# A second pair's sorted keys crossed batch by batch, and two value products moved in their down layers

## The chip, the cores and the metric

The kernel runs on one core of a Trainium2 chip. The metric is the time of one execution on the device in microseconds (us). Three timed runs of the kernel before gave 232.80, 232.84 and 232.96 us, median 232.84.

## The reference

Attention over sorted blocks, whose result goes through a feed-forward layer:

```
P = sort_net                              # (4 batches, 8 heads, 8, 8)
5 times: P = exp(P - rowmax); P /= row sums; P /= column sums
k_sorted, v_sorted = P applied to the 8 blocks of 96 rows of k and v
scores = q_block @ k_sorted_block^T / 8   # 96 x 96 for each block
attn   = softmax(scores)                  # minus the row's maximum
x      = attn @ v_sorted_block            # -> (3072 tokens, 512)
h = x @ w_in;  g = h * cos(h);  out = g @ w_out    # 512 -> 2048 -> 512
```

q, k and v are (4, 8, 768, 64); inputs and output are float32, the matmuls run in bf16.

## The kernel before

The 3,072 tokens are eight halves n = 0 to 7 of 384 tokens; half n belongs to batch n // 2. Each half has four units u of 96 tokens, one block of all eight heads. A unit's attention is written here as (n, u). Its steps: `qk_half`, `qk` or `batch(("sc", n, u), ...)` are the scores on TensorE with maximum and subtraction on VectorE; `expo(n, u)` is the exponential on ScalarE into one of three buffers `p_buf`, followed by a transpose of the probabilities into `pT` that SP issues as a DMA (L588), or that TensorE makes later where `on_pe` is set; `av(n, u)` is the product of `pT` with the sorted values on TensorE (L625, eight matmuls) and its norm on VectorE (L636, L638); the result is turned into `xT` by a DMA from SP (L644) or, with `on_pe`, on TensorE (`x_transpose`).

The feed-forward layer of half n is `moe_up(n)`, eight steps of eight matmuls (`h`, L669) with a sine on ScalarE and a product on VectorE (`gg`) behind each, and then the down layer: three tiles of 128 tokens, each in two halves of eight matmuls into one bank (`down(n, ts, half)`, L694). In `moe_down(n, slots, mid=...)` the six halves are e = 0 to 5. Attention of later halves is written between these steps: `slots[e]` runs behind half e, `mid` behind the fourth matmul of a half, `late` behind its fifth. The order in which these calls are written is the order on every engine; nothing reorders it. So an instruction that waits holds back all that stands behind it on its engine.

The batches go in two pairs: halves 0 to 3 and halves 4 to 7. For each, keys and values are first sorted by a matmul with P (`ks`, `vs`). Sorted keys of the second pair lie in `kT2`, a view of `kTs` with 128 partitions, three places and two batches. The sort fills places 0 and 2. `k_swap` fills place 1: it carries place 0 of the upper 64 partitions to the lower 64, and place 2 of the lower 64 to the upper 64, by two DMAs from SP (L421, L422). In what follows this is the crossing. Scores read the places hp and hp + 1 together, so they need it. Halves 4 and 5 read the first batch of `kT2`, halves 6 and 7 the second. The first pair's second batch has a crossing of its own, `k_swap(kT[1])`, of half the size of that of `kT2`.

SP's queue carries the crossings, the transposes of pT and xT, the turns of queries (`q_transpose_dma`, L149) and the stores of results, in the order written. GpSimd's queue carries the loads from memory; `p_hold` and `hold` make it wait for a transpose on SP's queue before more loads go out.

PSUM tiles of the pool `big` (three of two banks) hold scores, sorts, `h` and value products in turn, so a tile is written only when the engine that read its predecessor is through.

Of the kernel before, what the change touches and what calls it, by code (L numbers as in the profile page):

```python
# [18 lines left out]
def kernel(  # L19
# [15 lines left out]
    nc = tc.nc  # L35
    B, H, S, D = q.shape
# [110 lines left out]
    def q_transpose_dma(n):  # L147
        for e in range(2):
            nc.sync.dma_start_transpose(  # L149
                out=q_of(n, e)[:, :QW].rearrange("p (x c) -> p x c", c=blk),  # L150
                in_=q_zeroed(n)[:, e * QZ:(e + 1) * QZ])
# [36 lines left out]
    kT, kT2 = [kTs[:, :, 0], kTs[:, :, 2]], kTs[:, :, :2]  # L188
# [64 lines left out]
    V, A = nc.vector, nc.scalar  # L253

    def copy_on(eng, dst, src):
        if eng is nc.scalar:
            eng.copy(dst, src)  # L257
        else:
            eng.tensor_copy(dst, src)  # L259
# [151 lines left out]
    def k_sort_g(t0, eng, pool, tag):  # L411
        ps = pool.tile([128, 4, 4 * NB], FP32, name="ks", tag=tag)
        for t in range(4):
            k_products(ps, t, t0 + t, slice(0, 128), bds[1].rearrange("p x i -> p (x i)"),
                       pair)
        copy_on(
            eng, kT2[:, ::2, :, :, t0:t0 + 4].rearrange("p e b m t -> p b e m t"),
            ps.rearrange("p t (b e m) -> p b e m t", b=2, e=2))

    def k_swap(keys):  # L420
        nc.sync.dma_start(out=keys[:64, 1], in_=keys[64:, 0])  # L421
        nc.sync.dma_start(out=keys[64:, 1], in_=keys[:64, 2])  # L422

    def hold_keys():

        nc.gpsimd.tensor_copy(held[:], kT[1][:, 1, 0, :1])
# [106 lines left out]
    def batch(*parts, between=()):  # L533

        tiles = []
        for kind, *x in parts:
            ps = big.tile([128, 2, 512], FP32, name=kind, tag="big")
            tiles.append(ps)
            if kind == "sc":
                by_half(*x, ps)  # L540
            else:
                sort_eight(kind, x[0], ps)
        step(between)
        for (kind, *x), ps in zip(parts, tiles):
            if kind == "sc":
                s_t[tuple(x)] = sp.tile([blk, 2, H2, blk], FP32, name="s", tag="s")
                qk_reduce(*x, [0, 1], ps)
            else:
                place_eight(kind, *x[:1], ps, x[1])
# [132 lines left out]
    def store(n, ts, o_s, eng=nc.sync):  # L682
        r0 = n * TC + ts * 128
        eng.dma_start(out=out[r0:r0 + 128, :], in_=o_s[:])
# [4 lines left out]
    def down(n, ts, half, stores, mid=(), late=()):  # L689
        if half == 0:  # L690
            out_ps[ts] = acc.tile([128, Dm], FP32, name="o", tag="acc")
        o = out_ps[ts]
        for f in range(half * FC // 2, (half + 1) * FC // 2):
            nc.tensor.matmul(  # L694
                o[:], gt[n, f // 4][:, f % 4, ts * 128:(ts + 1) * 128], w_out_t[:, f, :],
                start=(f == 0), stop=(f == FC - 1))
            if f % (FC // 2) == FC // 4 - 1:
                step(mid)
            if f % (FC // 2) == FC // 4:
                step(late)  # L700
        if half == 0:
            return
        if stores is None:

            z = (n % 2 * 3 + ts) * 2 * Dm
            o_s = vbuf[:, z:z + 2 * Dm].bitcast(FP32)
        else:
            o_s = op.tile([128, Dm], FP32, name="o_s", tag="o_s")
        late = n > 0 and ts == TC // 128 - 1
        copy_on(V if late else A, o_s[:], o[:])  # L710
        if stores is None or stores == "held":
            kept[n, ts] = o_s
        else:
            store(n, ts, o_s, nc.sync if late else stores)

    def step(calls):
        for f, *args in calls:
            f(*args)

    def moe_up(n, slots=()):  # L720
        for fp in range(FC // 2):
            up(n, fp)
            step(slots[fp] if fp < len(slots) else ())

    def moe_down(n, slots=(), stores=nc.sync, mid={}, late=()):

        for e in range(2 * TC // 128):
            last = e == 2 * TC // 128 - 1
            down(n, e // 2, e % 2, stores, mid.get(e, ()), late if last else ())
            step(slots[e] if e < len(slots) else ())  # L730

    B, C = (big, "big"), (acc, "acc")
# [362 lines left out]
    kse(2, V)  # L1095
    kse(1, A)
    k_swap(kT[1])
    q_transpose(2, 0, (V, V), *C)
    q_transpose(2, 1, (V, V), *B)
# [34 lines left out]
    let_go(1, 0)  # L1134
    down(1, 1, 0, nc.sync)
    k_sort_g(16, A, *B)
    down(1, 1, 1, nc.sync, mid=[(av, 2, 0, True), (expo, 2, 3, True)])
    batch(("sc", 3, 0), ("ks", 1, A))
    p_hold(2, 2)
    for z in range(3, 6):  # L1140
# [12 lines left out]
         late=[(x_transpose, 2, 3, V, *B)])  # L1153
    q_transpose_dma(4)
    moe_up(2, [[(k_next,), (qk_half, 3, 1, 0)], [(k_next,)],
               [(k_next,), (qk_half, 3, 1, 1)], [(k_next,)],
               [(k_next,), (qk_half, 3, 2, 0)], [(k_next,)],
               [(qk_half, 3, 2, 1), (k_swap, kT2)]])

    expo(3, 1)  # L1160
    expo(3, 2)
    moe_down(2, [[(ones, 1), (batch, ("sc", 3, 3), ("vs", 0, A))],
                 [(expo, 3, 3), (batch, ("vs", 1, A), ("vs", 2, A)), (av, 3, 0)],
                 [(p_hold, 3, 3), (load_q, 5), (av, 3, 1)],
                 [(batch, ("sc", 4, 0), ("vs", 3, A), ("vs", 4, A))],
                 [(expo, 4, 0), (sine_next,)]],
             mid={3: [(av, 3, 2, True)], 4: [(av, 3, 3, True)], 5: [(x_transpose, 3, 2, V, *B, 3)]})
    q_transpose_dma(5)
    hold(q_turned[1])
    load_q(6)  # L1170
    moe_up(3, [[(w_next,), (qk_half, 4, 1, 0)], [(w_next,)],
               [(w_next,), (qk_half, 4, 1, 1)], [(w_next,)],
               [(w_next,), (qk_half, 4, 2, 0)], [(w_next,)],
               [(qk_half, 4, 2, 1)], [(qk, 4, 3)]])
    expo(4, 1)
# [4 lines left out]
             None, mid={3: [(av, 4, 1)], 4: [(av, 4, 2, True)]},  # L1180
             late=[(x_transpose, 4, 2, V, *B, 3)])
# [10 lines left out]
             None, mid={3: [(qk_av, 6, 1, 5, 2)]}, late=[(x_transpose, 5, 3, V, *B)])  # L1192
# [7 lines left out]
             None, mid={3: [(qk_av, 7, 1, 6, 2)]}, late=[(x_transpose, 6, 3, V, *B)])  # L1200
# [5 lines left out]
             mid={3: [(av, 7, 2)], 4: [(av, 7, 3, True)], 5: [(x_transpose, 7, 3, A, *B)]})  # L1206
# [45 lines left out]
```

## Time and profile before

| | |
|---|---|
| median of three timed runs | 232.84 us |
| the profiled execution | 232.49 us |
| its span, first to last instruction | 230.7 us |
| TensorE matmuls, busy | 222.9 us (97%) |
| TensorE's clock granted | 1.00 |
| DMA, share of the 16 engines from 97 to 112 us | 0.97 |
| read from memory, written | 27.27 MB, 6.29 MB |

By TensorE's order the up layer 1 begins at 56.6 us and the down layer 1 at 69.7; the up layer 2 at 84.4, the down layer 2 at 96.9 and the up layer 3 at 111.7. A row of the timeline gives the start, the time from there to the group's end, the engine, the line, the operation, the operands, the count, and in brackets the idle time ahead with what ended it. A matmul's end is modelled and includes its way through the array, so rows overlap a little, and the pitch of matmuls is read from starts. "PEld" is the weight load of a matmul, which waits for its data before the matmul does. "SPq" is SP's queue; its rows tell how long the issue of a transfer took, and "DMA to landing" the time from the start of the issue to the last of its data.

### The profile page before, as it was taken

What the parts mean: (1) busy time and instruction counts of PE and PEld (TensorE: products, weight loads), DVE (VectorE), ACT (ScalarE), POOL (GpSimd) and SP (SyncE); (2) the same over time, 40 slices, a digit from 0 to 9 for tenths busy, and PEclk for the clock granted to TensorE, in tenths of its full rate; (3) what the DMA queues carried; (4) which work ended last, traced back from release to release, by engine and by line L of the source; (5) the groups of instructions that cost most, each with busy time, mean ns of one, the idle gap of its engine ahead of it and who ended that gap; (6) DMA issues with size and microseconds to landing.
All of it is one profiled execution on the core that took longest, in us unless ns stands there. A gap on an engine that the chain in (4) does not pass through costs nothing.

```text
span 230.7 us, 5533 instructions
## 1 busy us (share of the span) xinstructions
PE 222.9 (97%) x2268; PEld 138.7 (60%) x2268; DVE 170.8 (74%) x291; ACT 154.4 (67%) x207; POOL 95.9 (42%) x121
## 2 busy tenths in 40 slices
PE   8788999999999999999999999999999999999994
PEld 3377898567765566655665456555655566556553
DVE  6769968978798778877589976997699769646700
ACT  5659877777889758796688466746674667716521
POOL 7989999299960289923609000800000000000000
PEclk9999999999999999999999999999999999999999
DMA  5999999994999699897979839964934450351012
GB/s 70 226 193 207 203 207 234 196 224 150 114 121 203 171 150 137 153 160 147 162 139 86 119 74 153 211 95 73 184 123 76 91 162 0 68 146 45 0 45 94
DMA packets 67673, 31.21 MB, mean 135 GB/s; under 512 B 56384, under 2 KB 63168, under 8 KB 67392
## 3 DMA queue, kind: packets, MB, share of 16 engines
q0 software_dynamic: 24048, 13.64, 44.2%
q1 hardware_dynamic: 43312, 17.02, 35.0%
q8 instruction: 18, 0.29, 0.5%
q10 hardware_dynamic: 288, 0.20, 0.3%
q14 instruction: 7, 0.06, 0.1%
HBM read 27.27 MB, written 6.29 MB: 145 GB/s over the span
## 4 chain that ended last, share of the span: by engine, by line
PE 85%; DMA 8%; POOL 2%; DVE 2%; issue 1%; ACT 0%; ACTq 0%; POOLq 0%
PE h L669 32%; PE o L694 29%; DMA q_mem<-in_q_dram 6%; PE h L857 5%; PE o L878 5%; PE av L625 3%; PE sc L438 3%; DMA pT<-p_buf 2%; PE o L1216 2%; PE ks L408 1%; POOL w_in_t L160 1%; PE sc L504 1%; PE xps L656 1%; PE vs L449 1%; PE qps L268 1%
## 5 line engine op out<-in xcount | busy, mean ns | idle before, releaser
L669 PE MATMUL h<-xT,w_in_t 128*128 128x384 bf16 x448 | 78.4, 326 | 0.0
L694 PE MATMUL o<-w_out_t,gg 128*128 128x512 bf16 x320 | 76.0, 379 | 0.0
L673 ACT ACTIVATE c<-h,half_pi 128x768 f32<-128x768 f32 x56 | 50.5, 902 | 26.0 <-PE h L669 25.0
L677 DVE TENSOR_TENSOR gg<-c,h 128x768 bf16<-128x768 f32 x56 | 52.7, 949 | 19.5 <-ACT c L673 19.5
L669 PEld LDWEIGHTS <-w_in_t 128*128 128x128 bf16 x448 | 42.2, 98 | 26.3 <-DVE xT L259 0.6
L694 PEld LDWEIGHTS <-gg 128*128 128x128 bf16 x320 | 29.0, 99 | 28.5
L179 POOL COPY vperm<-kv 64x768 bf16<-64x768 bf16 (+2 forms) x12 | 28.3, 2408 | 4.9 <-DMA kv<-in_v_dram 4.9
L570 ACT ACTIVATE p_buf<-s 96x768 bf16<-96x768 f32 x32 | 26.6, 842 | 5.3 <-DVE s L491 4.0
L491 DVE TENSOR_TENSOR s<-sc,mx 96x384 f32<-96x384 f32 (+1 forms) x33 | 24.3, 735 | 1.6
L489 DVE TENSOR_REDUCE mx<-sc 96x4 f32<-96x384 f32 (+1 forms) x33 | 24.0, 728 | 0.4 <-PE sc L504 0.4
L638 DVE TENSOR_TENSOR xn<-av,r 96x512 bf16<-96x512 f32 x32 | 22.0, 687 | 1.1
L129 POOL DMA_DIRECT2D kv<-in_q_dram x24 | 16.0, 675 | 0.7 <-issue 0.7
L257 ACT COPY kv<-o 128x512 f32<-128x512 f32 (+2 forms) x10 | 5.2, 524 | 14.1 <-PE o L694 11.5
L257 ACT CAST kTs<-ks 128x512 bf16<-128x512 f32 (+1 forms) x18 | 11.0, 630 | 5.3 <-PE ks L408 4.4
L636 DVE RECIPROCAL r<-av 96x8 f32<-96x8 f32 x32 | 6.4, 199 | 10.0 <-PE av L625 9.5
L878 PE MATMUL o<-w_out_t,gg 128*128 128x512 bf16 x48 | 11.7, 379 | 0.0
L129 POOL DMA_DIRECT2D q_mem<-in_q_dram x16 | 10.7, 692 | 1.8 <-DMA kv<-in_v_dram 1.4
L259 DVE COPY kv<-o 128x512 f32<-128x512 f32 (+1 forms) x5 | 3.1, 611 | 11.1 <-PE o L1216 8.5
L857 PE MATMUL h<-xT,w_in_t 128*128 128x192 bf16 x128 | 11.1, 246 | 0.0
L438 PE MATMUL sc<-kTs,q_turned 128*128 128x96 bf16 x152 | 11.1, 206 | 0.0
L857 PEld LDWEIGHTS <-w_in_t 128*128 128x128 bf16 x128 | 10.5, 98 | 0.0
L596 POOL CAST held<-q_turned 96x1 f32<-96x1 bf16 x2 | 0.4, 182 | 24.3 <-DMA q_turned<-q_mem 16.9
(134 smaller groups left out, 286.0 us busy)
## 6 DMA issues: line engine op xcount, KB each, us to landing
out_dram<-kv SPq DMA_DIRECT2D x12, 256.0 KB, 2.6
out_dram<-o_s SPq DMA_DIRECT2D x10, 256.0 KB, 3.5
w_in_t<-in_moe_w_in_dram POOLq DMA_DIRECT2D x4, 512.0 KB, 11.7
w_out_t<-in_moe_w_out_dram POOLq DMA_DIRECT2D x4, 512.0 KB, 12.4
kv<-in_k_dram POOLq DMA_DIRECT2D x2, 768.0 KB, 10.0
kv<-in_v_dram POOLq DMA_DIRECT2D x2, 768.0 KB, 13.4
pair<-in_k_dram POOLq DMA_DIRECT2D x2, 768.0 KB, 12.4
kv<-in_v_dram POOLq DMA_DIRECT2D x6, 256.0 KB, 5.6
```

Source lines behind the costliest of these rows:

```text
L129: nc.gpsimd.dma_start(out=q_heads[:, i, :, e], in_=src[:, ih * IC + i, :, e])
L179: nc.gpsimd.tensor_copy(dst, src)
L489: nc.vector.reduce_max(mx[:], scv, axis=AX.X)
L491: nc.vector.tensor_tensor(s, scv, mx.to_broadcast(list(s.shape)), op=ALU.subtract)
L570: nc.scalar.activation(p[:, :, :blk], s_t.pop((n, u)).rearrange("p e h c -> p (e h) c"), AF.Exp, scale=scale)
L638: nc.vector.tensor_tensor(xn.rearrange("p h e d -> p e h d"), avv[:, :, :, :D], r.to_broadcast([blk, 2, H2, D]), op=ALU.mult)
L669: nc.tensor.matmul(h[:, f2, :w], w_in_t[:, kk, f * 128:(f + 1) * 128], xT[n][:, kk], start=(kk == 0), stop=(kk == KC - 1))
L673: nc.scalar.activation(c[:], h[:, :, :w], AF.Sin, bias=half_pi[:, 0:1])
L677: nc.vector.tensor_tensor(gt[n, fp // 2][:, f:f + 2], c[:], h[:, :, :w], op=ALU.mult)
L694: nc.tensor.matmul(o[:], gt[n, f // 4][:, f % 4, ts * 128:(ts + 1) * 128], w_out_t[:, f, :], start=(f == 0), stop=(f == FC - 1))
L857: nc.tensor.matmul(o[:, part, f2 * w:(f2 + 1) * w], w_in_t[:, kk, f * 128:(f + 1) * 128], xT[0][:, kk, h * w:(h + 1) * w], start=(kk == 0) ...
L878: nc.tensor.matmul(out_ps[ts][:], gt[0, q][:, f % 4, ts * 128:(ts + 1) * 128], w_out_t[:, f, :], start=(f == 0), stop=(f == FC - 1))
```

## The change

Three calls are written in other places, and one is split. The crossing of `kT2` becomes two calls `k_swap_b(b2)`, each with one batch, half the bytes. The first batch crosses where both crossed before, at the end of the up layer 2; the second behind the scores (4, 1) in the up layer 3. The product av(2, 0) in the down layer 1 moves from behind the fourth matmul of its half to behind the fifth; expo(2, 3) stays. The product av(3, 0) in the down layer 2 moves from the end of the second half (e = 1) to the middle of the third (e = 2).

```diff
     def k_swap(keys):
         nc.sync.dma_start(out=keys[:64, 1], in_=keys[64:, 0])
         nc.sync.dma_start(out=keys[64:, 1], in_=keys[:64, 2])
+
+    def k_swap_b(b2):
+        k_swap(kT2[:, :, b2])
...
     k_sort_g(16, A, *B)
-    down(1, 1, 1, nc.sync, mid=[(av, 2, 0, True), (expo, 2, 3, True)])
+    down(1, 1, 1, nc.sync, mid=[(expo, 2, 3, True)], late=[(av, 2, 0, True)])
     batch(("sc", 3, 0), ("ks", 1, A))
...
                [(k_next,), (qk_half, 3, 2, 0)], [(k_next,)],
-               [(qk_half, 3, 2, 1), (k_swap, kT2)]])
+               [(qk_half, 3, 2, 1), (k_swap_b, 0)]])
 
     expo(3, 1)
     expo(3, 2)
     moe_down(2, [[(ones, 1), (batch, ("sc", 3, 3), ("vs", 0, A))],
-                 [(expo, 3, 3), (batch, ("vs", 1, A), ("vs", 2, A)), (av, 3, 0)],
+                 [(expo, 3, 3), (batch, ("vs", 1, A), ("vs", 2, A))],
                  [(p_hold, 3, 3), (load_q, 5), (av, 3, 1)],
                  [(batch, ("sc", 4, 0), ("vs", 3, A), ("vs", 4, A))],
                  [(expo, 4, 0), (sine_next,)]],
-             mid={3: [(av, 3, 2, True)], 4: [(av, 3, 3, True)], 5: [(x_transpose, 3, 2, V, *B, 3)]})
+             mid={2: [(av, 3, 0)], 3: [(av, 3, 2, True)], 4: [(av, 3, 3, True)], 5: [(x_transpose, 3, 2, V, *B, 3)]})
...
     moe_up(3, [[(w_next,), (qk_half, 4, 1, 0)], [(w_next,)],
-               [(w_next,), (qk_half, 4, 1, 1)], [(w_next,)],
+               [(w_next,), (qk_half, 4, 1, 1), (k_swap_b, 1)], [(w_next,)],
                [(w_next,), (qk_half, 4, 2, 0)], [(w_next,)],
```

On TensorE in the down layer 1, where av(2, 0) begins (`pT_1510` is its turned probabilities, `o_1582` the down layer's bank; lines behind the new helper stand three further down in the changed kernel). Before:

```order
L694 MATMUL o_1582<-w_out_t_97,gg_1423 128x512
L694 LDWEIGHTS gg_1423
L694 MATMUL o_1582<-w_out_t_97,gg_1423 128x512
L625 LDWEIGHTS pT_1510
L625 MATMUL av_1602<-vS_110,pT_1510 128x65
```

And now:

```order
L697 MATMUL o_1582<-w_out_t_97,gg_1423 128x512
L697 LDWEIGHTS gg_1477
L697 MATMUL o_1582<-w_out_t_97,gg_1477 128x512
L628 LDWEIGHTS pT_1510
L628 MATMUL av_1605<-vS_110,pT_1510 128x65
```

The first matmul of the half's second four, with the weights gg_1477, now stands ahead of the product.

On TensorE in the down layer 2, where av(3, 0) begins (its turned probabilities lie in `kv_87`; `vs_2024` is the value sort ahead of it). Before:

```order
L518 MATMUL vs_2024<-bd1_152,vperm_88 96x64
L518 LDWEIGHTS vperm_88
L518 MATMUL vs_2024<-bd1_152,vperm_88 96x64
L625 LDWEIGHTS kv_87
L625 MATMUL av_2044<-vS_110,kv_87 128x65
```

And now:

```order
L697 MATMUL o_2043<-w_out_t_97,gg_1785 128x512
L697 LDWEIGHTS gg_1785
L697 MATMUL o_2043<-w_out_t_97,gg_1785 128x512
L628 LDWEIGHTS kv_87
L628 MATMUL av_2049<-vS_110,kv_87 128x65
```

The first four matmuls of the third half, with gg_1785, have gone ahead of it; the other four, with gg_1831, follow it, and av(3, 1) stands behind them as before.

On SP's queue from the crossing in layer 2 (`pT_1947`, `pT_1950` and `pT_2005` are of the units (3, 1), (3, 2) and (3, 3)). Before:

```order
L421 DMA kTs_98<-kTs_98 64x3072
L422 DMA kTs_98<-kTs_98 64x3072
L588 DMA_TRANSPOSE pT_1947<-p_buf1_108 128x8x96
L588 DMA_TRANSPOSE pT_1950<-p_buf2_109 128x8x96
L684 DMA out_0_dram<-o_s_2001 128x512
L588 DMA_TRANSPOSE pT_2005<-p_buf0_107 128x8x96
```

The same stretch now has 64x1536 in the rows L421 and L422, and is else the same. The other batch's crossing stands later on that queue, behind the turn of query half 5 and ahead of the probabilities of unit (4, 1):

```order
L687 DMA out_0_dram<-o_s_2206 128x512
L149 DMA_TRANSPOSE q_turned1_95<-kv_87 128x16x96 x2
L421 DMA kTs_98<-kTs_98 64x1536
L422 DMA kTs_98<-kTs_98 64x1536
L591 DMA_TRANSPOSE pT_2406<-p_buf2_109 128x8x96
```

Two rows are new there; no other order on SP's queue differs.

## The prediction

> **What bounds the kernel now.** I read the page first, then the chain that ended last, then the waits of TensorE, then the timeline round the two waits that the change stands beside.
>
> ```profile
> PE 222.9 (97%) x2268; PEld 138.7 (60%) x2268; DVE 170.8 (74%) x291; ACT 154.4 (67%) x207; POOL 95.9 (42%) x121
> PE 85%; DMA 8%; POOL 2%; DVE 2%; issue 1%; ACT 0%; ACTq 0%; POOLq 0%
> PE h L669 32%; PE o L694 29%; DMA q_mem<-in_q_dram 6%; PE h L857 5%; PE o L878 5%; PE av L625 3%; PE sc L438 3%; DMA pT<-p_buf 2%; PE o L1216 2%; PE ks L408 1%; POOL w_in_t L160 1%; PE sc L504 1%; PE xps L656 1%; PE vs L449 1%; PE qps L268 1%
> ```
>
> TensorE is busy for 97% of the span and carries 85% of the chain. Of DMA's 8%, 6 are the first query load, which the change doesn't touch; 2 are a transfer "pT<-p_buf", which it does. A gain can only come out of the few places where TensorE stands still. Between 70 and 112 us, the stretch that the change works in, its weight loads waited for a transfer twice:
>
> ```profile
> PEld L625 <- DMA pT<-p_buf: 1.4, 2, 0.9
> ```
>
> Both are value products (L625) that wait for their turned probabilities pT. The first is av(2,0) in the down layer 1:
>
> ```profile
> 75.90 1.03 PE L694 MATMUL o<-w_out_t,gg 128*128 128x512 bf16 x4
> 76.93 0.43 PE L625 MATMUL av<-vS,pT 96*128 96x65 bf16 x8
> 77.20 0.38 PE L694 MATMUL o<-w_out_t,gg 128*128 128x512 bf16 x1
> ```
>
> The second is av(3,1), at the end of the third half of down layer 2; av(3,0) is the group ahead of it, which the change moves:
>
> ```profile
> 101.11 0.78 PE L518 MATMUL vs<-bd,vperm 64*128 64x64 bf16 x32
> 101.88 0.42 PE L625 MATMUL av<-vS,kv 96*128 96x65 bf16 x8
> 102.14 1.89 PE L694 MATMUL o<-w_out_t,gg 128*128 128x512 bf16 x8
> 104.44 0.43 PE L625 MATMUL av<-vS,pT 96*128 96x65 bf16 x8 [0.41 <-DMA pT<-p_buf]
> 104.71 1.03 PE L694 MATMUL o<-w_out_t,gg 128*128 128x512 bf16 x4
> 105.57 0.42 PE L625 MATMUL av<-vS,pT 96*128 96x65 bf16 x8
> ```
>
> A row's duration includes the tail of its last matmul, so the pitch comes from starts. Four down matmuls from 104.71 to the next group at 105.57 take 0.86, 0.216 each. At the first place four take 75.90 to 76.93 = 1.03: **0.17 us lost**. At the second, eight from 102.14 would be through at 102.14 + 1.73 = 103.87, and av(3,1) starts at 104.44: **0.57 us lost**. These 0.74 us are all that the change can aim at.
>
> **Part 1: av(2,0) one matmul later.** Its pT lands at 76.9 (72.8 + 4.1, rows below). With five matmuls ahead of it, it starts at 75.90 + 5 x 0.216 = 76.98, just past the landing, so TensorE no longer waits: what follows comes 0.17 earlier. ScalarE's exponential, which stays at its old place, is not delayed. The product itself ends 0.05 later, which matters on VectorE, the next engine to be late:
>
> ```profile
> 77.64 0.69 DVE L638 TENSOR_TENSOR xn<-av,r 96x512 bf16<-96x512 f32 x1
> 78.55 0.95 DVE L489 TENSOR_REDUCE mx<-sc 96x8 f32<-96x768 f32 x1 [0.22 <-PE sc L504]
> ```
>
> The norm of av(2,0) will end at 78.38 instead of 78.33; the maximum behind it waits for scores that come 0.17 earlier, so it can start at about 78.40. VectorE then runs on without a wait to the transposes on which TensorE waits for it. **Term 1: -0.15 us** (ends: 0 if VectorE gives it all back, -0.17).
>
> **Part 2: the crossing by batch, and why pT(3,1) is late.** On SP's queue the crossing of the second pair's keys stands right ahead of the pT of layer 2:
>
> ```profile
> 95.88 1.17 SPq L421 DMA_DIRECT2D kTs<-kTs  x1
> 97.10 0.58 SPq L422 DMA_DIRECT2D kTs<-kTs  x1
> 100.21 3.48 SPq L588 DMA_TRANSPOSE pT<-p_buf  x2
> ```
>
> ```profile
> kTs<-kTs SPq DMA_DIRECT2D x2, 384.0 KB, 5.6
> kTs<-kTs SPq DMA_DIRECT2D x2, 192.0 KB, 2.9
> ```
>
> The crossing of the first pair, 192 KB a transfer, landed in 2.9 us, that of the second, 384 KB, in 5.6. After the change each transfer here has 192 KB, so it should be through before pT(3,1) is issued at 100.21. SP itself wasn't late: the issue waits for the exponential. But is the crossing what holds pT(3,1)? The landings of four pT, one answer for each: av(2,0)'s, issued at 72.8, av(3,1)'s at 100.2, av(4,1)'s at 127.5, and av(3,2)'s at 101.7:
>
> ```profile
> L588 SPq DMA_TRANSPOSE pT<-p_buf x1: 1212/1212/1212, 72.8 to 72.8; - x1
> DMA to landing us min/median/max: 4.1/4.1/4.1
> ...
> L588 SPq DMA_TRANSPOSE pT<-p_buf x1: 1344/1344/1344, 100.2 to 100.2; - x1
> DMA to landing us min/median/max: 4.2/4.2/4.2
> ...
> L588 SPq DMA_TRANSPOSE pT<-p_buf x1: 1212/1212/1212, 127.5 to 127.5; - x1
> DMA to landing us min/median/max: 2.8/2.8/2.8
> ...
> L588 SPq DMA_TRANSPOSE pT<-p_buf x1: 2032/2032/2032, 101.7 to 101.7; - x1
> DMA to landing us min/median/max: 3.6/3.6/3.6
> ```
>
> The undisturbed one takes 2.8 us. The one at 72.8 took 4.1 with no crossing anywhere near it. What it shares with the one at 100.2 is in the queues' packets, here for 74.2 to 75.2, 101.6 to 102.6 and the clean 128.7 to 129.7:
>
> ```profile
> q1 hardware_dynamic: 409, 0.10, 217.6%
> q8 instruction: 1, 0.02, 5.8%
> ...
> q1 hardware_dynamic: 396, 0.10, 229.2%
> q8 instruction: 1, 0.02, 6.2%
> ...
> q1 hardware_dynamic: 756, 0.19, 102.8%
> ```
>
> In both late cases one packet of the instruction queue runs among the packets of the transpose, half as many packets start in the same microsecond, and they take twice the engines' time. In the clean case there is none. The page counts 18 such packets with 0.29 MB, 16 KB each; over TensorE's 4,536 matmuls and weight loads that makes 64 B an instruction, so I take them for TensorE's own code, which comes at fixed places of its program. The change leaves the number of instructions ahead of 101.6 as it is, so that packet will meet pT(3,1) again.
>
> The Trainium skill, "Runtime: NRT & Kernel Launch", section "Instruction fetch mechanics", says that the sequencer fetches the next 16 KiB block through its own DMA queue while it runs the present one, and that crossing a block is mostly hidden. The block size agrees with the 16 KB here; that it is hidden does not, by these rows, hold for a transpose in flight. By that rule the lateness would be the crossing's alone; that case is rival 1.
>
> So I price the crossing as the difference between the two late ones: 1.34 us of issue against 1.21, a landing of 4.2 against 4.1. **Term 2: -0.13 us** (ends: 0, and what the next thing to be late allows). That next thing is ScalarE, which clears the bank that av(3,1) writes:
>
> ```profile
> 98.05 1.28 ACT L570 ACT_TABLE_LOAD   x1
> 99.34 1.58 ACT L570 ACTIVATE p_buf<-s 96x768 bf16<-96x768 f32 x2
> 100.83 1.00 ACT L257 CAST pair<-vs 96x1024 bf16<-96x1024 f32 x1
> 102.95 1.93 ACT L257 CAST pair<-vs 96x1024 bf16<-96x1024 f32 x2
> ```
>
> The first of the two casts at 102.95, at 1.0 each, ends near 103.95, so av(3,1) can't start before about 104.0 on before's clock: at most 0.44 of the 0.57 can go. And pT(3,2) lands at 101.7 + 3.6 = 105.3, only 0.3 ahead of its product at 105.57, so unless it too comes earlier the third product gives back what is over that.
>
> **Part 3: av(3,0) four matmuls later.** Between the value sort and av(3,1) stand the same eight matmuls and eight products as before, only in another order. The start of av(3,0) at 101.88 was 0.05 behind the end of the cast at 101.83, so a few hundredths of waiting go there, but all of it runs into the wait for pT(3,1). Its norm on VectorE comes later by those four matmuls, but the transfer behind it was queued on SP after pT(3,3) anyway. **0.** By itself it is worth something only where pT(3,1) comes early.
>
> **Part 4: the later batch's crossing in layer 3.** SP gets two more issues behind the turn of query half 5 and ahead of pT(4,1), at 0.58 to 1.17 us each by the rows at 97.10 and 95.88. SP is idle there:
>
> ```profile
> L149 SPq DMA_TRANSPOSE q_turned<-kv x2: 1435/1636/1837, 116.7 to 118.4; - x2
> DMA to landing us min/median/max: 3.9/4.0/4.2
> ...
> 128.32 0.64 PE L504 MATMUL sc<-kTs,q_turned 64*128 64x96 bf16 x16
> ```
>
> The turn is issued by 120.2 and SP's next transfer is pT(4,1) at 127.5, so up to 2.3 us fit. The crossed keys of that batch are read first by scores of half 6, in down layer 4. Cover: seven idle microseconds of SP; without them, pT(4,1) would be issued up to 2.3 later. **0.**
>
> **Sum.** From 70 us on everything hangs on TensorE, which waits for nothing else of this size, so the shift should last to the end: -0.15 - 0.13 = **-0.28 us**. The profiled execution took 232.49 us (230.7 of span, 1.8 round it), so it would come to 232.21. The median of the three timed runs is 0.35 above the profiled one; carried over, 232.84 - 0.28 = **232.56 us**, 0.12% less. A measurement of this kernel can tell about 0.2%, 0.47 us, from no change, so the forecast is a gain too small to tell.
>
> **Rivals.**
> 1. *The crossing alone held pT(3,1).* For it: it overlaps in time, and 5.6 us of landing against 2.9. Against it: the pT at 72.8. pT(3,1) would land 2.8 after 100.21, at 103.0; ScalarE's cast then sets the start, -0.44. With term 1 -0.59: 232.25, and about 232.4 if pT(3,2) holds the third product. Chance 0.15.
> 2. *The crossing costs nothing, or the saved wait reappears.* The instruction packet alone sets the landing, or VectorE returns term 1. Gain 0 to 0.15: 232.7 to 232.84. Chance 0.22.
> 3. *Slower: the later crossing holds the turn of half 5.* Place: SP's transfers at 116.7 to 121. The turn lands at 118.38 + 4.2 = 122.5 and is read at 128.32, so it decides only when the landing slips by over 5.8 us; each further microsecond costs one on TensorE. To lose over 0.47 net of both terms, it must slip by 5.8 + 0.28 + 0.47 = 6.55 us: 233.31. Against it: the crossing stands behind the turn on the same queue, and the slips seen here are 2.7 (5.6 against 2.9) and 1.4 us (4.2 against 2.8). Chance 0.08.
>
> **How the numbers follow.** Forecast (gain 0.15 to 0.45) 0.55; rivals 0.15, 0.22, 0.08. Rival 1 lies on both sides of the 0.47 bound, mostly past it when it holds: with some scatter between sets of runs, faster 0.14; slower 0.08; same 0.78. The range takes in the forecast, rivals 1 and 2 and about 0.15 of scatter, since the three runs lie 0.16 apart: 232.2 to 233.0.
>
> **What would show it.** Part 1: five matmuls ahead of av(2,0) and its start 0.86 + 0.22 behind theirs, everything at 84 us 0.15 earlier. Part 2: both crossing transfers landing in about 3 us, the instruction packet still among pT(3,1)'s, a landing of 4.0 to 4.1, and a wait of some 0.4 to 0.5 still ahead of av(3,1). Part 4: no wait of TensorE at 128 or 150. I am wrong if pT(3,1) lands in 2.8 (rival 1), or if the instruction packet has moved off it, or onto another transfer that is read soon.

## The result, and the profile after

| kernel | runs | median us | lowest to highest |
|---|---|---|---|
| before | 7 | 232.96 | 232.05 to 233.22 |
| changed | 7 | 231.89 | 231.61 to 232.00 |

The ratio is 0.9951 with a 95% interval of 0.9938 to 0.9964: a gain of 1.07 us where 0.28 was forecast, and a time below the range given. The profiled execution of the changed kernel took 231.61 us (229.8 of span).

The chain that ended last, and the waits of TensorE's weight loads between 70 and 112 us, in the profile after (lines behind the new helper stand three further down, so L625 is now L628, L588 is L591):

```profile
PE 90%; DVE 3%; POOL 2%; issue 1%; ACT 1%; POOLq 0%; ACTq 0%
```

```profile
PEld L628 <- DMA pT<-p_buf: 0.6, 2, 0.3
```

"DMA pT<-p_buf" has gone from the chain, and the longest wait for a turned pT is 0.3 us instead of 0.9. The two that are left are weight loads of av(2,0) (0.30) and av(3,2) (0.28), and the matmuls behind them start no later for it; at av(3,1) none is left. The timeline of TensorE at the two places:

```profile
75.72 1.24 PE L697 MATMUL o<-w_out_t,gg 128*128 128x512 bf16 x5
76.80 0.42 PE L628 MATMUL av<-vS,pT 96*128 96x65 bf16 x8
77.06 0.81 PE L697 MATMUL o<-w_out_t,gg 128*128 128x512 bf16 x3
...
102.35 0.42 PE L628 MATMUL av<-vS,kv 96*128 96x65 bf16 x8
102.60 1.03 PE L697 MATMUL o<-w_out_t,gg 128*128 128x512 bf16 x4
103.67 0.41 PE L628 MATMUL av<-vS,pT 96*128 96x65 bf16 x8
103.92 1.03 PE L697 MATMUL o<-w_out_t,gg 128*128 128x512 bf16 x4
104.78 0.42 PE L628 MATMUL av<-vS,pT 96*128 96x65 bf16 x8
```

At the first place five matmuls take 75.72 to 76.80 = 1.08, their own pitch: the 0.17 us are gone, as forecast. At the second, av(3,1) (103.67) follows its four matmuls with 0.2 us of standstill instead of 0.57 behind eight, and the third product doesn't give it back. What holds av(3,1) now is ScalarE's cast, the first of these two, which ends near 103.6:

```profile
102.60 1.93 ACT L257 CAST pair<-vs 96x1024 bf16<-96x1024 f32 x2
```

SP's queue, and the landings of the crossing's second transfer and of pT(3,1):

```profile
96.59 1.15 SPq L421 DMA_DIRECT2D kTs<-kTs  x1
97.78 0.59 SPq L422 DMA_DIRECT2D kTs<-kTs  x1
99.87 3.24 SPq L591 DMA_TRANSPOSE pT<-p_buf  x2
```

```profile
L422 SPq DMA_DIRECT2D kTs<-kTs x1: 587/587/587, 97.8 to 97.8; - x1
DMA to landing us min/median/max: 3.1/3.1/3.1
...
L591 SPq DMA_TRANSPOSE pT<-p_buf x1: 1910/1910/1910, 99.9 to 99.9; - x1
DMA to landing us min/median/max: 3.1/3.1/3.1
```

pT(3,1) lands in 3.1 us, not in the 4.1 forecast. What the transfers moved shows why. The rows are GB/s in 40 equal slices and the packets by queue, first before from 100 to 104.5 us, then after from 99 to 104:

```profile
GB/s 382 218 437 273 164 273 328 109 382 109 0 0 55 162 316 155 159 180 191 71 7 0 2 7 7 11 9 9 9 11 184 282 101 132 164 166 189 168 216 275
...
q8 instruction: 1, 0.02, 1.4%
```

```profile
GB/s 270 49 295 98 344 442 393 320 156 0 0 0 0 0 0 0 59 162 162 160 147 215 152 29 100 289 98 1 0 0 0 0 43 164 164 164 164 201 268 256
...
q8 instruction: 1, 0.02, 1.5%
```

Before, the slices up to 101.1 are mostly the crossing; then the transposes begin (first data at 101.39), the code packet starts (at 101.61 by its record, when the crossing's last packet ends), and from 102.25 to 103.4 next to nothing moves: ten slices of 0.11 us. After, the crossing is out by 100.1, the packet starts there (100.12 to 101.30), before the transposes' first data at 101.05, and they run through. The packet is the same one: 1,269 weight loads had started before it in the kernel before, 1,239 after. It came 30 weight loads earlier in the program.

**Two stretches** carry the rest of this document. Stretch 1 runs from the start of the key sort (L408) ahead of the last half around av(2,0) to the start of the scores behind it; stretch 2 from the start of the scores (3,3) to that of the scores (4,0). Outside them, between two weight loads of the same number, no two unpadded profiles differ by over 0.02 us from 28 us on (unpadded: without the idle matmuls that some experiments add); in the first 28 us executions of one kernel scatter by some 0.4.

| | stretch 1 | stretch 2 |
|---|---|---|
| before, first profile | 78.16 - 75.68 = 2.48 | 106.79 - 98.75 = 8.04 |
| changed, first profile | 77.81 - 75.50 = 2.31 | 106.00 - 98.40 = 7.60 |

So the two profiles differ by 0.17 + 0.44 in the places aimed at, by 0.18 in the first 28 us, which the change doesn't touch, and by 0.08 behind TensorE's last weight load. The rest of the 1.07 between the medians is not in this pair of profiles at all.

### The profile page after: what moved, and what is told of

It is laid out like the page before. It is cut to its first block, busy times and chain, and to the rows that moved or that the text cites. A ratio compares the mean times of both kernels' runs of the same rounds, so it can differ in the third digit from the quotient of the medians.

```text
span 229.8 us, 5513 instructions
## 1 busy us (share of the span) xinstructions
PE 220.8 (96%) x2245; PEld 138.7 (60%) x2268; DVE 170.8 (74%) x291; ACT 154.4 (67%) x207; POOL 96.1 (42%) x121
## 4 chain that ended last, share of the span: by engine, by line
PE 90%; DVE 3%; POOL 2%; issue 1%; ACT 1%; POOLq 0%; ACTq 0%
PE h L672 32%; PE o L697 30%; PE h L860 5%; PE o L881 4%; PE av L628 4%; PE sc L441 3%; PE ks L408 2%; PE o L1219 2%; PE pps L838 1%; PE sc L507 1%; PE xps L659 1%; PE vs L785 1%; PE vs L452 1%; PE qps L268 1%; PE xps L847 1%
## 5 line engine op out<-in xcount | busy, mean ns | idle before, releaser
L697 PE MATMUL o<-w_out_t,gg 128*128 128x512 bf16 x303 | 73.7, 379 | 1.0 <-issue 0.3
L881 PE MATMUL o<-w_out_t,gg 128*128 128x512 bf16 x45 | 11.2, 379 | 0.2
```

What stands on the lines that cost most here:

```text
L697: nc.tensor.matmul(o[:], gt[n, f // 4][:, f % 4, ts * 128:(ts + 1) * 128], w_out_t[:, f, :], start=(f == 0), stop=(f == FC - 1))
L881: nc.tensor.matmul(out_ps[ts][:], gt[0, q][:, f % 4, ts * 128:(ts + 1) * 128], w_out_t[:, f, :], start=(f == 0), stop=(f == FC - 1))
```

## The experiments

**Theory A**: TensorE's code packet waits behind the crossing's packets on its DMA engine. A whole crossing holds it back until it falls among pT(3,1)'s packets; a halved one lets it through before them. The rivals: the moved products earn the gain (M); the crossing's own bytes hold pT(3,1) (rival 1 of the prediction); not the bytes but the size of the transfers counts (F).

### The two parts apart

The crossing by batch alone, with both products at their old places (against the changed kernel):

```diff
-    down(1, 1, 1, nc.sync, mid=[(expo, 2, 3, True)], late=[(av, 2, 0, True)])
+    down(1, 1, 1, nc.sync, mid=[(av, 2, 0, True), (expo, 2, 3, True)])
...
-                 [(expo, 3, 3), (batch, ("vs", 1, A), ("vs", 2, A))],
+                 [(expo, 3, 3), (batch, ("vs", 1, A), ("vs", 2, A)), (av, 3, 0)],
...
-             mid={2: [(av, 3, 0)], 3: [(av, 3, 2, True)], 4: [(av, 3, 3, True)], 5: [(x_transpose, 3, 2, V, *B, 3)]})
+             mid={3: [(av, 3, 2, True)], 4: [(av, 3, 3, True)], 5: [(x_transpose, 3, 2, V, *B, 3)]})
```

> The crossing goes by batch, both value products stay at their old places. Theory A (the crossing's bytes push TensorE's code packet of 16 KB back until it meets the transpose of pT(3,1)): the packet comes near 100 us instead of 101.6, pT(3,1) lands in 2.8 to 3.2 instead of 4.2, and the 0.57 us at the second place fall to 0.1 to 0.2; the 0.17 at the first place stays. Time 0.4 to 0.6 us under before, ratio 0.9975 to 0.9983. Theory B (the moved products carry the gain): no change, ratio 1.000.

The two moves alone, with the crossing whole, are the other half of the diff.

> Both value products move, both batches still cross at the old place. Theory A: the packet still comes near 101.6 and pT(3,1) still lands in 4.0 to 4.2; only the 0.17 us at the first place goes: ratio 0.9993. Theory B: the whole gain, ratio 0.995 to 0.996.

| kernel | runs | median us | ratio to before (233.41, 23 runs) | stretch 1 | stretch 2 |
|---|---|---|---|---|---|
| crossing by batch alone | 5 | 232.29 | 0.9953 (0.9940 to 0.9966) | 2.64 | 7.58 |
| moves alone | 11 | 233.50 | 1.0006 (0.9997 to 1.0014) | 2.31 | 9.31 |

The crossing by batch earns the gain; the moves alone earn nothing. With the crossing by batch the packet came at 100.61 and pT(3,1) landed 3.1 us after its issue, as theory A expected; with the moves alone they read 102.20 and 5.5, later than its 101.6 and 4.0 to 4.2. In their profile (234.0 us, 0.5 above the median) the moves gain 0.17 in stretch 1 and lose it in stretch 2, where TensorE then waits the longer:

```profile
105.81 0.43 PE L628 MATMUL av<-vS,pT 96*128 96x65 bf16 x8 [1.73 <-DMA pT<-p_buf]
```

Two things did not fit theory A as first put: the gain of 1.12 us is larger than the 0.4 to 0.6 expected, and the stretch 2 of 9.31 us with the whole crossing is worse than the 8.04 of the first profile of before.

### More instructions ahead, from the start of the program

To move the code packet against pT(3,1), the 14 idle matmuls of 512 columns at the start became 30 of 240 in the kernel before, and 122 of 59 in the changed one:

```diff
-    keep_warm(14, big.tile([128, 512], FP32, name="idle", tag="big"))
+    keep_warm(30, big.tile([128, 512], FP32, name="idle", tag="big"), 240)
...
+    keep_warm(122, big.tile([128, 512], FP32, name="idle", tag="big"), 59)
```

> The kernel before with 16 more matmuls in its warm-up at the start, each narrower, with the same number of columns in all: every later instruction of TensorE stands 32 places further on, so each code packet is asked for 32 instructions earlier in the work; crossing and products are untouched. Theory A in the form 'where the packet falls decides': asked for near 99 instead of 100.4; if an engine serves it between the crossing's packets, pT(3,1) lands near 2.9 and the second place gains 0.4 to 0.57, and pT(2,0), whose packet comes at 72 instead of 74.3, lands in 2.8 and the first place gains 0.17: ratio 0.9968 to 0.998. If the packet must wait until the crossing has drained: pT(3,1) still 4.2, ratio 0.9993. Rival (the crossing's bytes hold pT(3,1), the packet is harmless): pT(3,1) 4.2 in any case, no change, ratio 1.000.

> The changed kernel with 108 more, narrower matmuls in its warm-up, the same columns in all: 216 more instructions, so each code packet is asked for 40 instructions later (256 to a packet). Theory A: the packet that came at 100.1 comes near 101.0 to 101.5, among the packets of pT(3,1), which lands in 3.9 to 4.2 again although the crossing is halved; the wait ahead of av(3,1) is 0.5 to 0.9 and the time is 0.3 to 0.7 us over that of the changed kernel, unless the first place gains its 0.1 from a packet that has moved off pT(2,0). Ratio to before 0.9965 to 0.999. Rival (crossing's bytes alone): pT(3,1) stays at 3.0, ratio 0.995 as for the change.

Measured were 234.54 (ratio 1.0045, 1.0033 to 1.0057) and 233.39 us (1.0010, 0.9992 to 1.0029). Both lie above all that either side expected. The totals can't be read: every code packet moved, those of the first 28 us too, and both profiles reach stretch 1 some 1.1 to 1.9 us later than the unpadded ones of the same kernel. The places can. In the padded kernel before, the packet near pT(2,0) came at 74.20, 0.06 us ahead of that transfer's issue; pT(2,0) landed in 2.8 us, and stretch 1 took 2.31 though av(2,0) stood at its old place. So without the packet the first wait is gone, whatever the order. At the second place the packet came at 102.24, again behind crossing packets (nine still to start), and stretch 2 is 8.20. In the padded changed kernel the packet, asked for 108 weight loads earlier than its like in the changed kernel, came at 105.02, among pT(3,1)'s packets though the crossing is halved:

```profile
GB/s 394 393 369 320 78 160 164 215 227 215 229 158 154 119 96 180 358 172 102 57 31 10 0 6 10 8 10 10 8 10 246 357 426 442 344 508 270 254 289 293
...
q8 instruction: 1, 0.02, 1.1%
```

```profile
107.14 0.43 PE L628 MATMUL av<-vS,pT 96*128 96x65 bf16 x8 [1.64 <-DMA pT<-p_buf]
```

The slices (103 to 108 us, 0.125 each) show the same standstill from 105.5 to 106.75; pT(3,1) landed 5.2 us after its issue and stretch 2 took 9.23. So a halved crossing does not save the place once the packet falls there. Here pT(3,1) was also issued only 1.9 us behind the crossing, so part of the 5.2 is the crossing's.

### The changed kernel and one move at a time

> The changed kernel once more, beside three variants of it. Theory A (halving the crossing lets TensorE's 16 KB code packet through earlier, ahead of the transfer of pT(3,1) instead of in the middle of it): ratio 0.995, crossing landing in 3.2 to 3.5 us, code packet at 100.0 to 100.7 us right behind the crossing's first transfer, pT(3,1) landing in 3.0 to 3.1 us. Theory M (the two moved value products earn a part of it): the same time, but then both variants with only one of the moves lie above it.

Both batches' crossings in layer 2, in four transfers of half the size:

```diff
-               [(qk_half, 3, 2, 1), (k_swap_b, 0)]])
+               [(qk_half, 3, 2, 1), (k_swap_b, 0), (k_swap_b, 1)]])
...
-               [(w_next,), (qk_half, 4, 1, 1), (k_swap_b, 1)], [(w_next,)],
+               [(w_next,), (qk_half, 4, 1, 1)], [(w_next,)],
```

> The changed kernel, but the later batch's two crossing transfers stand right behind the first batch's in up layer 2: same bytes on the queue as before the change, in half as large transfers. Theory A: the code packet is again served only when all of the crossing's packets ahead of it are gone, at 101.3 to 102.3 us, among pT(3,1)'s packets, which land 4.0 to 5.5 us after the issue; the time goes back to before, ratio 0.999 to 1.001. Rival F (the form: 3 KB packets instead of 6 KB let the other queues in, whatever their number): packet at 100 to 100.7, pT(3,1) landing in 3.1, ratio 0.995.

The changed kernel with av(3,0) put back, and with av(2,0) put back (the diff lines of the first experiment, one at a time):

> The changed kernel with av(3,0) put back ahead of the third half of down layer 2; crossing by batch and the later av(2,0) stay. Theory A: 0.995, as the changed kernel, and no wait of more than 0.05 us ahead of av(2,0). Theory M, if it is av(3,0) that earns: 0.997 or more, with the lost time ahead of av(3,1).

> The changed kernel with av(2,0) put back to the middle of its half; crossing by batch and the later av(3,0) stay. Theory A: 0.17 us above the changed kernel, ratio 0.9955 to 0.996, from the wait ahead of av(2,0), which stays at 0.15 to 0.3 us. Theory M, if it is av(2,0) that earns all: 0.999.

| kernel | runs | median us | ratio to before (233.35, 17 runs) | stretch 1 | stretch 2 |
|---|---|---|---|---|---|
| changed, again | 6 | 232.11 | 0.9948 (0.9928 to 0.9967) | 2.53 | 7.59 |
| all crossings in layer 2, halved | 10 | 232.46 | 0.9958 (0.9943 to 0.9973) | 2.37 | 7.89 |
| av(3,0) put back | 6 | 231.94 | 0.9943 (0.9924 to 0.9962) | 2.43 | 7.60 |
| av(2,0) put back | 8 | 232.24 | 0.9950 (0.9933 to 0.9966) | 2.39 | 7.60 |

The medians don't part the moves; the stretches do. Stretch 2 is 7.58 to 7.60 in all five unpadded profiles whose crossing is by batch, with av(3,0) at either place: that move is worth nothing. Stretch 1 scatters with the landing of pT(2,0), which has a code packet of its own. In the second profile of the changed kernel it landed 4.3 us after its issue instead of 4.1, and TensorE waited there again, for the later product too:

```profile
PEld L628 <- DMA pT<-p_buf: 0.5, 1, 0.5
```

With av(3,0) put back 0.12 us were lost at this place too, where theory A expected 0.05 at most. The six profiles with av(2,0) at its old place and a late pT(2,0) (2.48, 2.54, 2.62, 2.64, 2.39, 2.49; those of before and of the padded kernel below among them) have a mean of 2.53, the nine with the later one (2.31, 2.53, 2.43, 2.37, 2.31, 2.31, 2.31, 2.46, 2.37) of 2.38: the move is worth **0.15 us**, on average. The two kernels padded from the start are left out, since there pT(2,0) landed in 2.8; stretch 1 took 2.31 in both.

The kernel with all crossings in layer 2 missed theory A's 0.999 to 1.001. Its packet came at 101.0, between the two times that were expected and 0.24 us ahead of pT(3,1)'s first data; pT(3,1) landed in 4.0 us, but that cost only 0.3 of stretch 2. That was left for the last experiment.

### The packet moved off and on, close to the place

48 idle matmuls of 8 columns ahead of av(2,3) at 81 us in the kernel before, 84 in the changed one (its lines read alike): only code packets behind that point move.

```diff
-        av_products(n, u)
+        av_products(n, u, 48 if (n, u) == (2, 3) else 0)
...
-        keep_warm(fill, a[:, 0], 256)
+        keep_warm(fill, a[:, 0], 8 if n == 2 else 256)
```

> The kernel before, whole crossing, with 48 tiny idle matmuls (8 columns) ahead of av(2,3) at 81 us: 96 instructions more on TensorE, 1.5 to 2.5 us of pure filling, so only the place at av(3,1) is read, not the total. The code packet that used to be asked for at about 100.4 us is asked for 48 weight loads earlier, ahead of the crossing. Theory A (the packet among pT(3,1)'s is what makes it late; the crossing does so only by holding the packet back): no packet inside pT(3,1), landing in 2.8 to 3.2 us, wait ahead of av(3,1) 0.2 us or less, though the crossing is whole. Rival 1 (the crossing's own bytes hold pT(3,1)): landing still 4 us or more and a wait of 0.4 us or more.

> The changed kernel, crossing by batch, with 84 tiny idle matmuls (8 columns) ahead of av(2,3) at 81 us, 2.5 to 4 us of pure filling; only the place at av(3,1) is read. The code packet after the one at 100 us is asked for 84 weight loads earlier and should fall into pT(3,1)'s transfer, with the crossing halved. Theory A: pT(3,1) lands 4.0 to 5.5 us after its issue, the transposes in flight stand still for 1.3 to 1.5 us, and TensorE waits 0.5 us or more ahead of av(3,1). Rival 1: crossing halved, so landing in 2.8 to 3.1 and no wait.

In the first, the packet came at 97.80, ahead of the first data of the crossing (97.84). The landing of pT(3,1), and the timeline of av(3,1):

```profile
L588 SPq DMA_TRANSPOSE pT<-p_buf x1: 1224/1224/1224, 101.4 to 101.4; - x1
DMA to landing us min/median/max: 2.8/2.8/2.8
```

```profile
105.18 0.42 PE L625 MATMUL av<-vS,pT 96*128 96x65 bf16 x8
```

The crossing is whole, and yet pT(3,1) lands in 2.8 us, TensorE doesn't wait for it, and stretch 2 is 107.52 - 99.93 = **7.59**, that of the changed kernel. What was moved is the place of the code packet, at a cost of 1.15 us for the filling (and the next packet now falls among the transposes of xT, at 107.2). One reservation: here the crossing was issued 4.7 us ahead of pT(3,1), in before 3.3 to 4.3, so its own tail came earlier against pT(3,1) too: 0.9 us behind the issue, in the first profile of before 1.4.

In the second the packet missed its mark. It came at 105.95, when pT(3,1) had landed (2.8 us), and fell among the packets of pT(3,2):

```profile
L591 SPq DMA_TRANSPOSE pT<-p_buf x1: 1235/1235/1235, 103.7 to 103.7; - x1
DMA to landing us min/median/max: 4.4/4.4/4.4
```

```profile
108.20 0.43 PE L628 MATMUL av<-vS,pT 96*128 96x65 bf16 x8 [0.71 <-DMA pT<-p_buf]
```

No crossing was near it (its last data at 100.6), and the transfer took 1.6 us more, TensorE waited at av(3,2) instead, and stretch 2 was 8.47. So the packet alone makes a transpose late; it did so at pT(3,2) here, as at pT(2,0) above.

### The kernel before, profiled again

> The kernel before, profiled once more. Theory A with a lucky first profile (the profiled execution of before, 232.49 us, was one in which the crossing ran through at once, so that the code packet came at 101.6 and pT(3,1) landed in 4.2): an ordinary execution, 233.2 to 233.6 us, shows the packet at 102.2, still with crossing packets behind it, pT(3,1) landing in 4.3 to 5.5 us and 1.0 us or more of wait ahead of av(3,1). Rival (the rest of the measured gain comes from elsewhere in the program): the place at av(3,1) reads as in the first profile, landing 4.2 and a wait of about 0.6, and the extra time lies at another place.

> The same once more, a third profile of the kernel before: if the time is 233.2 us or more, theory A expects the landing of pT(3,1) at 4.3 to 5.5 us, the rival 4.2 and the loss elsewhere; if it is 232.5 or so, theory A expects the reading of the first profile.

They took 233.63 and 234.07 us. Timeline, SP's queue and landings of the first of them:

```profile
105.51 0.43 PE L625 MATMUL av<-vS,pT 96*128 96x65 bf16 x8 [1.24 <-DMA pT<-p_buf]
```

```profile
96.90 1.12 SPq L421 DMA_DIRECT2D kTs<-kTs  x1
98.08 0.59 SPq L422 DMA_DIRECT2D kTs<-kTs  x1
100.45 3.88 SPq L588 DMA_TRANSPOSE pT<-p_buf  x2
```

```profile
L422 SPq DMA_DIRECT2D kTs<-kTs x1: 587/587/587, 98.1 to 98.1; - x1
DMA to landing us min/median/max: 6.7/6.7/6.7
...
L588 SPq DMA_TRANSPOSE pT<-p_buf x1: 2042/2042/2042, 100.5 to 100.5; - x1
DMA to landing us min/median/max: 5.0/5.0/5.0
```

Stretch 2 is 107.86 - 98.99 = 8.87 here and 9.14 in the other, stretch 1 2.54 and 2.62. The first profile of before, 8.04, was a lucky execution, as theory A had it: its crossing was issued 100.21 - 95.88 = 4.33 us ahead of pT(3,1); in these two it was 3.55 and 3.30. The code packet came at 101.90 and 102.43, with 12 and 11 of the crossing's 128 packets still to start, and the last of those ended at 104.19 and 104.72. pT(3,1) landed 1.27 and 1.26 later.

### All crossings in layer 2, three times more

> Both batches' crossings in layer 2 in half as large transfers, profiled again. Read: how long the crossing is issued ahead of pT(3,1), and TensorE's stretch from the scores of unit (3,3) to those of unit (4,0) (8.0 to 9.1 us before, 7.6 with the changed kernel, 7.89 in the first profile of this one). Theory A (bytes and order alone set it): with a lead of 3.2 to 3.6 us the stretch is 8.5 to 9.2. Rival F (the form matters): 7.6 to 8.0 at every lead.

> The same again, with the same two readings: theory A 8.5 to 9.2 us at a lead of 3.2 to 3.6, about 7.9 at a lead of 4.0 or more; rival F 7.6 to 8.0 at every lead.

> The same a third time, same numbers: theory A's stretch goes with the lead, rival F's doesn't.

| | crossing issued ahead of pT(3,1) | code packet at | last crossing packet | pT(3,1) lands | stretch 2 |
|---|---|---|---|---|---|
| before, first profile | 4.33 | 101.61 | 101.61 | 104.40 | 8.04 |
| before, second | 3.55 | 101.90 | 104.19 | 105.46 | 8.87 |
| before, third | 3.30 | 102.43 | 104.72 | 105.98 | 9.14 |
| moves alone | 3.24 | 102.20 | 104.51 | 105.77 | 9.31 |
| halved, all in layer 2 | 4.02 | 101.00 | 102.88 | 104.10 | 7.89 |
| the same, second | 3.58 | 100.92 | 103.18 | 104.40 | 8.28 |
| the same, third | 3.72 | 100.52 | 103.16 | 104.37 | 8.06 |
| the same, fourth | 3.28 | 100.73 | 103.10 | 104.32 | 8.08 |
| changed, first | 3.28 | 100.12 | 100.15 | 102.94 | 7.60 |
| changed, second | 3.32 | 100.56 | 100.63 | 103.36 | 7.59 |

Neither theory is right as it was put. With the whole crossing the stretch follows the lead, with the halved one hardly. The same bytes in halved transfers cost a mean of 8.08 instead of 8.68, so 0.60 of the gain is the form; the other 0.48, down to 7.60, is the second batch gone from the place. That split is rough: it rests on four and three profiles, which scatter by 0.4 and 1.1, and the medians of the runs above (233.35, 232.46, 232.11) give 0.89 and 0.35. The wait at av(3,1) in the fourth of them:

```profile
104.36 0.43 PE L628 MATMUL av<-vS,pT 96*128 96x65 bf16 x8 [0.49 <-DMA pT<-p_buf]
```

The table shows a rule for the cases with crossing packets still to start at the packet: pT(3,1) lands 1.2 to 1.3 us behind the last of them. In these seven rows the packet started 0.1 to 1.0 us ahead of pT(3,1)'s first data, so among the crossing's packets; theory A had put it among the transpose's. Of the whole table only the first profile of before, with no crossing packet left to start, has it there. So the packet makes pT(3,1) late in two ways: it stops the transpose itself, or it delays the crossing's tail ahead of it. From first data to last the whole crossing took 3.9 us in the first profile of before (97.70 to 101.61), and 5.5 to 5.6 in the other two and with the moves alone, where the packet stands inside it. With halved transfers the code packet starts 0.9 to 1.9 us earlier, while 44 to 90 crossing packets are still to come in the three later profiles (12 in the first), so the tail behind it ends at 103 instead of 104.5.

## Why the prediction was wrong

**What bounds the kernel, and where a gain can come from**: right. The gain came out of the two places, and nothing behind them moved by more than 0.1 us. That "these 0.74 us are all that the change can aim at" holds for the first profile alone.

**Term 1, -0.15**: right in size as a mean (0.15), by the mechanism named; single executions scatter from 2.31 to 2.53 with the landing of pT(2,0). That the product "no longer waits" held in the first profile of the changed kernel and not in the second.

**Term 2, -0.13: the step that failed.** Two sentences of it. First: the packet "comes at fixed places of its program", so it "will meet pT(3,1) again". The place was not fixed: the crossing that the change shortens was what held the packet back. In before and with the moves alone it came with 1,269 to 1,276 weight loads started, in all five unpadded profiles with the crossing by batch with 1,238 or 1,239. That count is where it is asked for, since it was the same with av(2,0) put back, where the crossing's last packet had ended at 99.92 and the code packet came at 100.85. The two late transposes compared, at 72.8 and 100.2, were rightly put down to one cause, but the price of the crossing was then read as the difference of their landings, 0.1 us, as if packet and crossing were independent. Second: the sum was made on the profiled execution, and the 0.35 up to the median was "carried over", as though it lay where the change does not reach. Most of it lay at this place: 8.04 there against a mean of 8.68 in three profiles. With it, term 2 measures 8.68 - 7.60 = **-1.08**, and with term 1 -1.23, against 1.07 and 1.24 between the medians of the two sets of runs with both kernels.

**ScalarE's cast as the limit, 0.44**: right. 8.04 - 7.60 = 0.44, every profile with an early pT(3,1) stops at 7.58 to 7.60, and in the changed kernel av(3,1) starts 0.07 us behind the cast's end near 103.6.

**pT(3,2) and the third product**: it landed 2.8 us after its issue in the changed kernel and gave nothing back.

**Part 3**: right, 0. "By itself worth something only where pT(3,1) comes early" was too hopeful: with av(3,0) at its old place stretch 2 is the same 7.60.

**Part 4**: right, 0; from the scores (4,0) to TensorE's last weight load the kernels agree within 0.02 us, so the second batch's crossing in layer 3 costs nothing.

**Rival 1** named the landing (2.8 to 3.1) and the place, with too small a gain, 0.44 there, since it too was sized on the first profile. Its cause, that the crossing alone held pT(3,1), is part of the truth. By the table, pT(3,1) lands behind the crossing's tail; but that tail is late where a code packet stands in it. With the packet moved away, the whole crossing cost nothing at a lead of 4.7 us. The Trainium skill, "Runtime: NRT & Kernel Launch", section "Instruction fetch mechanics", holds crossing a code block to be mostly hidden. Of TensorE's own stream no run here shows otherwise; for the transposes that the fetch meets it has a price: 4.4 us of landing for pT(3,2) in the padded changed kernel, with no crossing near, against 2.8.

**Rival 2** (no gain at the second place) and **rival 3** (a later turn of half 5) did not come about: the turn landed at 122.5 us in both first profiles.

**What stays open.** How much of an ordinary execution's 1.08 the crossing would cost without a packet: a whole crossing at a lead of 3.3 us with no packet near was not seen. An estimate: with 3.9 us from first data to last, as in the first profile of before, the crossing of the second would have ended at 98.68 + 3.9 = 102.6 and pT(3,1) landed 1.3 behind, at 103.9, ahead of the 104.2 that the cast allows there; by that it would cost nothing. Why the transposes stand still until 103.4 in that first profile, when the packet has ended at 102.60, no run shows. Why halved transfers let the packet in earlier: the Trainium skill, "DMA: Bandwidth & Descriptors", section "Queues, rings and completion order", says that a DMA engine changes between queues only at packet boundaries, in turn. In four of the five profiles with the whole crossing and the packet behind it, the packet did start within 0.05 us of the landing of the first transfer (101.86 and 101.90, 102.40 and 102.43, 102.15 and 102.20, 102.19 and 102.24), which speaks for waiting out a whole transfer, but no run isolates it.

## What to carry to other kernels

Where one profile of the kernel before lies below the median by as much as the gain that is sought, profile it again before pricing a wait: the difference may sit at the very place. A transfer that looks guilty only by overlap can act through something small that has to wait for it, so ask what else waits there, and treat a packet that falls at a fixed place of the program as movable by whatever is ahead of it. Here, cutting a bulk copy into smaller transfers and sending late what is needed late kept the transposes that follow it early; whether it does elsewhere has to be measured there.

## What the runs showed of the hardware

- A 16 KB packet of the instruction queue that started 0.8 to 2.2 us behind the issue of a transpose of pT, with no crossing near, made it land 4.0 to 4.4 us after its issue, against 2.8 (pT(2,0) in fifteen profiles, pT(3,2) in the padded changed kernel). At pT(3,1) in the first profile of before, such a packet was followed by 1.1 us in which next to nothing moved (102.25 to 103.4). One that started within 0.3 us of the issue, ahead of the first data and with no crossing packet still to start, left it at 2.8 to 3.1 (five profiles with the crossing by batch), and one 2.4 us or more behind the issue at 2.8 (with av(3,0) put back: issue at 135.57, packet at 138.02).
- Such a packet itself takes 0.88 to 1.85 us, and came later with the whole crossing ahead of it: by 30 to 38 weight loads of TensorE's program, some 1.3 us between the second profiles of before and of the changed kernel.
- The same bytes, two crossing transfers of 384 KB cut into four of 192 KB, let a packet behind them start at 100.5 to 101.0 us instead of 101.6 to 102.4.
- Executions of the kernel before differ by 1.6 us (232.49 to 234.07 in three profiles), 1.1 of it at one wait.
